# Turning the rows of hn with VectorE blocks and DMA writes instead of TensorE transposes

## The chip, the core and the metric

The kernel runs on one core of one Trainium2 chip. The core has five engines, each with an instruction queue of its own that it works through in order: TensorE (PE in the profile) multiplies matrices and transposes, VectorE (DVE) and ScalarE (ACT) work on rows of up to 128 partitions, GpSimd (POOL) does elementwise work beside them, and SyncE (SP) issues most of the DMA transfers. ScalarE can issue DMA transfers too; they stand in its queue between its computations. TensorE writes to PSUM, eight banks of 128 x 512 floats; everything else lives in SBUF or, outside the core, in DRAM. The metric is the device time of one execution in microseconds (us), as the median of several runs.

## The reference

All values are float32. With S = 2048 rows, D = 512 columns, 32 heads of 16 and a gate of 688 columns, the reference computes

```python
h  = x + A(layernorm(x))             # attention with wqkv, softmax, wo
h2 = h + B(layernorm(h))             # gated MLP that mixes rows

def B(x):
    z  = gelu(x @ w_in)              # 2048 x 1376
    z1 = z[..., :688]
    z2 = layernorm(z[..., 688:])
    g  = w_sp @ z2 + b_sp[:, None]   # 2048 x 2048 weights over the rows
    return (z1 * g) @ w_out
```

The change concerns the step from layernorm(h) to x @ w_in: the product needs the rows of layernorm(h), called hn, turned, with the 512 columns on the partitions.

## The kernel before

A float32 product is made of three products of float32r parts (`mm3`, lines 107 to 110): a value is split into hi, the rounded value, and lo, the rest (`split`, lines 97 to 105), and hi x hi, hi x lo and lo x hi are added in PSUM.

The work has four stages. First the rows of x are normalized and projected to q, k and v, which go to DRAM. Then comes attention, with scores, exponentials and weighted sums in an order that is written out by hand as strings (lines 42 to 57); its results o and their sums r go to DRAM too. The last 22 units of attention follow the string `FINAL` (line 44, `play_final`). In it the letter G is half a unit of scores with their exponentials, V a weighted sum, and H one product of the output projection: 36 letters H make the rows of h for the first three row blocks (`more_h`, lines 863 to 884), twelve products for each.

A row block has 128 rows. `h_rows` (line 616) says in which order the 16 row blocks are taken: 0, 1, 2, 8, 9, 10, 3, 11, 4, 12 and so on. I call the place in this order the row's index.

The middle stage begins at line 999 and has 16 rounds, k = 0 to 15 (line 1071). Before, round k does this, in the order of the program:

- `make_h` for the row with index k + 3 (while there is one): twelve products of o with wo on TensorE (L643), x added by VectorE (L653), the sum stored to h_scr by SP (L655), statistics (L657).
- `turn` for the row with index k + 1 (L1015): four 128 x 128 transposes of hn on TensorE into PSUM, then the split, hi on ScalarE (L100) and lo on VectorE (L105), into one of two places of the tile hT. The row with index 0 is turned ahead of the loop.
- `scale_h`: mean and variance of the new row, and one over its deviation, a chain of small VectorE operations.
- `make_z`, three pieces of the 1376 columns, each twelve products of hT with w_in (L108 to L110), followed by the GELU on ScalarE (L1034). Between the first two pieces stands the split of o for the row with index k + 4; between the second and third, VectorE's statistics of z2 (L1094) and hn of the new row, which ScalarE makes (L1097).
- `gate_z`: ScalarE issues the store of z1 (L1041), VectorE turns the statistics into scales (L1043, L119 to L135, L666), ScalarE applies them (L1046) and issues the store of z2 (L1047). SP issues `load_o` for the row with index k + 5: o, four loads of r (rc), and x (L623 to L629); GpSimd multiplies o by r (L630). For the row blocks 8 to 15, GpSimd also prepares parts of the later products (L1058 to L1066).

From line 999 on, the program's order is the order of every engine's queue; in attention this holds for all engines but GpSimd. SP works ahead of TensorE wherever its buffers and data allow. DMA transfers report their end through eight semaphores, which all issues use in turn; an issue waits until the transfer that used its semaphore before has landed.

PSUM in the middle stage: one bank for the products of h (`ph`), two for the transposes (`pt`), five for the pieces of z (`ps`).

The fourth stage mixes the rows with w_sp (seven products in place of eight, on sums and differences of blocks) and projects with w_out. It takes z1 and z2 from DRAM again.

Of the kernel before, what the change touches and what calls it, by code (L numbers as in the profile page):

```python
# [18 lines left out]
P = 128  # L19
# [41 lines left out]
def block_kernel(ctx: ExitStack, tc: tile.TileContext, x, wqkv, wo, w_in, w_sp4, b_sp, w_out, out):  # L61
# [28 lines left out]
    o_scr = dram.tile([D, S], F32, name="o_scr")  # L90
    r_scr = dram.tile([H, S], F32, name="r_scr")
    h_scr = dram.tile([S, D], F32, name="h_scr")
    z_scr = [dram.tile([S, FH], F32, name=f"z{i}_scr") for i in range(2)]
    s_scr = dram.tile([HB, P, HB, P], F32, name="s_scr")
    g_scr = [dram.tile([3, P, FC], F32, name=f"g{p}_scr") for p in range(HB)]
# [518 lines left out]
    wi4 = w_in.rearrange("(a p) c -> p a c", p=P)  # L614

    h_rows = [0, 1, 2, HB, HB + 1, HB + 2] + [sb + HB * i for sb in range(3, HB) for i in range(2)]
    os_, o2s, xrs, hns, hTs = {}, {}, {}, {}, {}

    def load_o(sb):

        c = slice(sb * P, (sb + 1) * P)
        o = e2.tile([P, DB, P], F32, name="o")
        nc.sync.dma_start(o, o_scr[:, c].rearrange("(d p) s -> p d s", p=P))  # L623
        rc = e2.tile([P, DB, P], F32, name="rc")
        for d in range(DB):
            nc.sync.dma_start(rc[:, d, :], r_scr[8 * d:8 * d + 8, c].rearrange(
                "h (o s) -> h o s", o=1).to_broadcast([8, DH, P]))
        xrs[sb] = e2.tile([P, D], F32, name="xr", bufs=3)
        nc.sync.dma_start(xrs[sb], x[c, :])  # L629
        nc.gpsimd.tensor_mul(o, o, rc)  # L630
        os_[sb] = o

    def split_o(sb, eh="act", el=None):
        o = os_.pop(sb)
        o2s[sb] = [e2.tile([P, DB, P], F32R, name=f"o2{i}", bufs=1) for i in range(2)]
        split(o2s[sb][0], o2s[sb][1], o, eh, el)
# [14 lines left out]
    def add_h(sb, acc, between=lambda: None):  # L651
        h = xrs[sb]
        nc.vector.tensor_add(h, acc, h)  # L653
        between()
        nc.sync.dma_start(h_scr[sb * P:(sb + 1) * P, :], h)  # L655
        hst[sb] = e2.tile([P, 6], F32, name="st")
        nc.vector.bn_stats(hst[sb], h)  # L657

    def scale_h(sb):
        mv = e2.tile([P, 2], F32, name="mv")  # L660
# [21 lines left out]
    with ExitStack() as at:  # L682
# [127 lines left out]
        def play_final(units):  # L810


            half = []
            for x in FINAL:
                if x == "G":
                    if not half:
                        unit = units.pop(0)
                        half.extend([unit, new_pt(), 0])
                        if unit[2] == 6 and sums_:
                            invert()  # L820
                        if len(units) in (7, 5):
                            load_o(h_rows[(7, 5).index(len(units)) + 3])
                    unit, pt, p = half
                    for step in score(unit, p, pt):
                        step()
                    half[2] += 1
                    if p:
                        waiting.append([(unit, pt, PLACES), 0])
                        half.clear()
                elif x == "V":  # L830
                    unit, *rest = waiting.pop(0)[0]
                    weigh(unit, *rest)
                    if unit[2] == NB - 1:
# [29 lines left out]
        def more_h(k):  # L863

            for _ in range(k):
                if not pieces:
                    sb = h_rows[len(hns)]
                    acc = later[0].tile([P, 512], F32, name="h")
                    pieces.extend([sb, acc, h_products(sb, acc)])
                sb, acc, products = pieces  # L870
                next(products)
                made[0] += 1
                if made[0] % (3 * DB):
                    continue
                pieces.clear()
                after = h_rows[len(hns) + 1]
# [5 lines left out]
                hns[sb] = e2.tile([P, D], F32, name="hn", bufs=3)  # L882
                nc.vector.tensor_scalar(hns[sb], xrs.pop(sb), mv[:, 0:1], rs,
                                        op0=ALU.subtract, op1=ALU.mult)

        made = [0]
        units = [(hg, qb, kb) for hg in range(HG) for qb in range(NQ) for kb in range(NB)]
# [3 lines left out]
        with tc.manual_schedule(engines={E.PE, E.Activation, E.DVE, E.SP}):  # L891
            end = len(units) - 2 * LEAD
            for n in range(0, end, 2):
                hg, qb, kb = units[n]
                if hg + 1 < HG and n % 64 < 24 and n % 4 == 0:
                    load_k(hg + 1, [n % 64 // 4])
                if hg + 1 < HG and n % 64 < 12 and n % 4 == 2:
                    load_d(hg + 1, [n % 64 // 4])
                if hg + 1 < HG and n % 64 == 30:
                    load_v(hg + 1)  # L900
                if kb == 2 and n // NB + 3 < HG * NQ:
                    load_q(n // NB + 3)
# [18 lines left out]
            load_o(h_rows[2])  # L921
            maxima.close()
# [77 lines left out]
    with ExitStack() as mid:  # L1000
        m2 = mid.enter_context(tc.tile_pool(name="mid_2", bufs=2))
        zs, zst = {}, {}
        hT = wc.tile([P, 2, 2, DB, P], F32R, name="hT", tag="w2")
        ph = mid.enter_context(tc.tile_pool(name="mid_ph", bufs=1, space=PSUM))
        pt = mid.enter_context(tc.tile_pool(name="mid_pt", bufs=2, space=PSUM))
        ps = mid.enter_context(tc.tile_pool(name="mid_ps", bufs=5, space=PSUM))

        turned = [0]

        def turn(sb):  # L1010

            hn = hns.pop(sb)
            tp = pt.tile([P, DB, P], F32, name="tp")
            for d in range(DB):
                nc.tensor.transpose(tp[:, d, :], hn[:, d * P:(d + 1) * P], ident)  # L1015
            hTs[sb] = [hT[:, i, turned[0] % 2] for i in range(2)]
            turned[0] += 1
            split(hTs[sb][0], hTs[sb][1], tp, "act")

        def new_z(sb):  # L1020
            zs[sb] = [m2.tile([P, FH], F32, name=f"z{i}", bufs=1 + 4 * i) for i in range(2)]
# [45 lines left out]

        w = [Slot(wc, f"w{i}") for i in range(3)]
        row = dict(enumerate(h_rows))
        turn(row[0])  # L1070
        for k in range(NB):
            sb, new = row[k], row.get(k + 3)
            if new is not None:
                make_h(new, (ph if k else ps).tile([P, 512], F32, name="acc"))
            if k + 1 < NB:
                turn(row[k + 1])
            if new is not None:
                mv, rs = scale_h(new)
                nb = minus_mean(e2, mv, rs)
# [9 lines left out]
            make_z(sb, *chunks[0])  # L1089
            if k + 4 < NB:  # L1090
                split_o(row[k + 4])
            make_z(sb, *chunks[1])
            for c in range(2):
                nc.vector.bn_stats(zst[sb][:, c, :], zs[sb][1][:, c * FC:(c + 1) * FC])  # L1094
            if new is not None:
                hns[new] = e2.tile([P, D], F32, name="hn", bufs=3)
                nc.scalar.activation(hns[new], xrs.pop(new), AF.Identity, bias=nb, scale=rs)  # L1097
            for c in chunks[2:]:
                make_z(sb, *c)
            hTs.pop(sb)  # L1100
            gate_z(sb, lambda: k + 5 < NB and load_o(row[k + 5]))
            if not k:
                invert()
            if k == NB - 5:
# [354 lines left out]
```

## Time and profile before

| what | us |
|---|---|
| median of 3 runs | 1803.45 (1803.33 to 1804.55) |
| the profiled execution's own time | 1802.38 |
| its span, first to last instruction | 1800.6 |
| the middle stage, round 0 to round 15 | 1351.36 to 1513.97 of the span |

The profile is of one execution. Its page gives the busy time of each engine; a chain of waits that is followed back from the last instruction; and groups of equal instructions with what their engine waited for. The timeline lists single instructions: start in us from the beginning of the span, duration, engine, line of the kernel, operation, and the tiles that are written and read (`hT<-tp`: hT from tp). In brackets stands the engine's idle time before it and what ended it. ACTq and SPq are the queues of ScalarE and SP; a `DMA_DIRECT2D` there is the issue of a transfer, not the transfer itself, and isn't counted as busy time. Rounds 0 to 12 of the middle stage last 10.67 us each, with round 0 a little longer; rounds 13 and 14 have no row of h to make and last 7.91.

### The profile page before, as it was taken

The numbers are of one execution on the slowest core, as the hardware profiler recorded it, in microseconds if no ns is written. First come the engines' busy times: TensorE is split into PE (matmuls) and PEld (weight loads), VectorE is DVE, ScalarE is ACT, GpSimd is POOL, SyncE is SP. The second block draws the span as 40 slices with busy tenths as digits, with TensorE's granted clock in tenths as the row PEclk, the third lists the DMA queues.
The fourth block names the chain that finished last, engine by engine and source line by source line (L and its number), as shares of the span: only waits on it lengthen the run. The fifth ranks groups of instructions, "written<-read, shape, count | busy, mean of one in ns | idle before, by whom it ended". The sixth has DMA issues, their size and how long they took to land.

```text
span 1800.6 us, 36057 instructions
## 1 busy us (share of the span) xinstructions
PE 1793.1 (100%) x13371; PEld 1050.6 (58%) x13371; DVE 1500.0 (83%) x3034; ACT 1378.4 (77%) x2674; POOL 218.4 (12%) x299
## 2 busy tenths in 40 slices
PE   9999999999999999999999999999999999999999
PEld 6876444444444444444444444444448889999998
DVE  6487999999999999999999999999936676778664
ACT  3224999999999999999999999999994445334231
POOL 2241000011010100000000000000110754001111
PEclk9999999999999999999999999999999999999999
DMA  6677111221120111021012011100134554668562
GB/s 199 192 194 182 43 26 27 49 56 30 36 59 19 51 39 26 20 50 35 14 36 44 24 30 38 26 15 15 40 74 143 168 176 151 216 208 278 184 197 91
DMA packets 148184, 157.54 MB, mean 87 GB/s; under 512 B 63032, under 2 KB 93256, under 8 KB 146664
## 3 DMA queue, kind: packets, MB, share of 16 engines
q1 hardware_dynamic: 143224, 143.82, 29.6%
q10 hardware_dynamic: 4752, 11.41, 1.6%
q8 instruction: 105, 1.72, 0.4%
q14 instruction: 71, 0.58, 0.1%
q0 software_dynamic: 32, 0.01, 0.0%
HBM read 99.69 MB, written 54.56 MB: 86 GB/s over the span
## 4 chain that ended last, share of the span: by engine, by line
PE 99%; DVE 1%; DMA 0%; issue 0%; ACT 0%; DVEq 0%
PE pv L726 30%; PE s L700 10%; PE s L237 9%; PE m L700 9%; PE m L237 7%; PE acc L108 6%; PE acc L110 6%; PE acc L109 6%; PE g L110 4%; PE g L109 4%; PE g L108 4%; PE acc L643 2%; PE tp L1319 1%; PE h L643 1%; PE acc L1340 0%; PE tp L1015 0%
## 5 line engine op out<-in xcount | busy, mean ns | idle before, releaser
L704 ACT ACTIVATE pt<-s 128x512 f32<-128x512 f32 (+1 forms) x1149 | 668.5, 632 | 3.4 <-PE s L700 3.0
L726 PE MATMUL pv<-pt,vst 128*32 128x256 f32 (+1 forms) x6048 | 595.2, 467 | 0.0
L242 DVE TENSOR_REDUCE mx<-s 128x1 f32<-128x512 f32 x826 | 539.6, 682 | 42.3 <-PE s L237 34.4
L704 ACT ACTIVATE pt<-m 128x512 f32<-128x512 f32 x855 | 500.3, 616 | 0.2 <-PE m L700 0.2
L242 DVE TENSOR_REDUCE mx<-m 128x1 f32<-128x512 f32 x682 | 452.3, 682 | 28.3 <-PE m L237 21.2
L700 PE MATMUL s<-qst,kst 50*128 50x512 f32 x1193 | 418.5, 437 | 0.0
L237 PE MATMUL s<-kst,qst 48*128 48x512 f32 x963 | 343.7, 421 | 0.0
L700 PE MATMUL m<-qst,kst 50*128 50x512 f32 x855 | 340.1, 440 | 0.0
L237 PE MATMUL m<-kst,qst 48*128 48x512 f32 x794 | 290.8, 423 | 0.0
L700 PEld LDWEIGHTS s<-qst,kst 50*128 50x128 f32 x1193 | 187.4, 184 | 145.0 <-DVE mx L242 91.0
L726 PEld LDWEIGHTS pv<-pt,vst 128*32 128x32 f32 x6048 | 120.4, 108 | 217.6 <-issue 208.5
L700 PEld LDWEIGHTS m<-qst,kst 50*128 50x128 f32 x855 | 146.2, 184 | 129.4 <-DVE mx L242 88.9
L237 PEld LDWEIGHTS s<-kst,qst 48*128 48x128 f32 x963 | 166.8, 184 | 40.4 <-issue 12.8
L237 PEld LDWEIGHTS m<-kst,qst 48*128 48x128 f32 x794 | 137.1, 184 | 41.7 <-issue 15.2
L247 ACT ACTIVATE ab<-s 128x512 f32<-128x512 f32 x167 | 100.4, 601 | 14.2
L102 POOL CAST mparts<-nm 128x16 fp32r<-128x16 f32 x32 | 6.3, 196 | 861.3 <-DVE nm L255 861.3
L251 DVE CUSTOM_DVE_ANT_0 ab<-s,ab 128x512 f32<-128x512 f32 x137 | 93.2, 680 | 5.1 <-PE s L237 5.1
L955 ACT ACTIVATE ws<-a 128x512 fp32r<-128x512 f32 x80 | 45.7, 621 | 48.7 <-PE g L110 23.8
L251 DVE CUSTOM_DVE_ANT_0 ab<-m,ab 128x512 f32<-128x512 f32 x112 | 76.2, 680 | 4.9 <-PE m L237 4.9
L237 PE MATMUL s<-dst,qst 48*128 48x512 f32 x167 | 79.6, 477 | 0.0
L1034 ACT ACTIVATE z<-acc 128x464 f32<-128x464 f32 (+2 forms) x64 | 27.5, 456 | 63.5 <-PE acc L110 63.5
L108 PE MATMUL acc<-wi,hT 128*128 128x464 f32 (+2 forms) x196 | 72.8, 371 | 0.0
(219 smaller groups left out, 2586.9 us busy)
## 6 DMA issues: line engine op xcount, KB each, us to landing
a<-in_w_sp SPq DMA_DIRECT2D x80, 256.0 KB
qst<-q_scr SPq DMA_DIRECT2D x192, 64.0 KB
z_scr<-z ACTq DMA_DIRECT2D x32, 344.0 KB
kst<-k_scr SPq DMA_DIRECT2D x42, 256.0 KB
k_scr<-part SPq DMA_DIRECT2D x16, 512.0 KB
q_scr<-part SPq DMA_DIRECT2D x16, 512.0 KB
z<-z_scr SPq DMA_DIRECT2D x14, 344.0 KB
b<-z_scr SPq DMA_DIRECT2D x24, 172.0 KB
```

The costliest lines, as they stand in the source:

```text
L108: nc.tensor.matmul(ps, lh, rh, start=first, stop=False)
L109: nc.tensor.matmul(ps, lh, rl, start=False, stop=False)
L110: nc.tensor.matmul(ps, ll, rh, start=False, stop=last)
L237: nc.tensor.matmul(acc, q[r, p, c], keys[r, p], start=True, stop=True)
L242: nc.vector.reduce_max(at(t, e if t else e - 1), acc, axis=AX.X)
L247: nc.scalar.activation(ab[0], acc, AF.Relu)
L251: nc.vector.tensor_tensor_reduce(ab[0], acc, ab[0], 1.0, LOW, ALU.add, ALU.max, at(0, 0))
L643: yield nc.tensor.matmul(acc, o2[b][:, d, :], wo2[a][:, d, :], start=i == 0, stop=i == 3 * DB - 1)
L700: nc.tensor.matmul(out, kst[hg % 2][r, p, kb * P:(kb + 1) * P], qst[hg * NQ + qb][r, p, :], start=True, stop=True)
L704: nc.scalar.activation(out, scores, AF.Exp, scale=DH ** -0.5)
L726: nc.tensor.matmul(pv[0][32 * j:32 * j + 32, cols], vst[hg % 2][:, c:c + 32], pt[:, places[t, p], cols], start=kb == 0, stop=kb == NB - 1 ...
L955: nc.scalar.activation(hi, src, AF.Copy)
```

## The change

TensorE's transposes of hn go. In their place each row block is turned in two steps. VectorE transposes the 128 x 512 tile in blocks of 32 x 32 (`flip`): afterwards, row 32 i + r and columns 32 j to 32 j + 31 of the tile z hold column 32 j + r of rows 32 i to 32 i + 31. Four DMA writes, one for each i, put these pieces of 32 floats (128 bytes) at their places in a DRAM tile ht_scr, whose rows are the columns of hn; 2048 pieces in all. Later SP fetches the turned block from there in one transfer (`fetch_turned`), and it is split into hi and lo as before (`split_turned`).

For the rows with index 0 to 2, which are made in attention, VectorE transposes and SP issues the writes right behind the store of h. Rows 0 and 1 are fetched in `play_final`, at the units with 13 and 3 left, and row 0 is split by VectorE when the second row of h is complete. For the rows made in rounds 0 to 12, ScalarE's queue issues the four writes, behind the store of z2, and SP fetches the row with index k + 2 at the end of round k, behind `load_o`. The split for the row with index k + 1 stands in round k between the first and second piece of z, behind the split of o. The turned copy shares the three buffers of hn. The five PSUM banks for z become seven, as no bank holds transposes any more.

```diff
+    ht_scr = dram.tile([D, S], F32, name="ht_scr")
...
+    def flip(sb, hn):
+
+        z = e2.tile([P, D], F32, name="hz", tag="hn", bufs=3)
+        nc.vector.transpose(z, hn)
+        q = 32
+
+        def write(e=nc.sync):
+            for i in range(P // q):
+                c = sb * P + q * i
+                e.dma_start(ht_scr[:, c:c + q].rearrange("(j r) c -> r j c", r=q),
+                            z[q * i:q * i + q, :].rearrange("r (j c) -> r j c", c=q))
+
+        return write
+
+    def fetch_turned(sb, pool, **slot):
+
+        raws[sb] = pool.tile([P, DB, P], F32, name="ht", **slot)
+        nc.sync.dma_start(raws[sb], ht_scr[:, sb * P:(sb + 1) * P].rearrange("(a p) s -> p a s", p=P))
+
+    def split_turned(sb, eh=None):
+
+        hTs[sb] = [hT[0][:, i, turns[0] % 2] for i in range(2)]
+        turns[0] += 1
+        split(hTs[sb][0], hTs[sb][1], raws.pop(sb), eh)
...
+                        if len(units) in (13, 3):
+                            fetch_turned(h_rows[(13, 3).index(len(units))], e2, tag="rc")
...
+                if made[0] == 6 * DB:
+                    split_turned(h_rows[0])
...
-                nc.vector.tensor_scalar(hns[sb], xrs.pop(sb), mv[:, 0:1], rs,
+                hn = e2.tile([P, D], F32, name="hn", bufs=3)
+                nc.vector.tensor_scalar(hn, xrs.pop(sb), mv[:, 0:1], rs,
                                         op0=ALU.subtract, op1=ALU.mult)
+                flip(sb, hn)()
...
-        pt = mid.enter_context(tc.tile_pool(name="mid_pt", bufs=2, space=PSUM))
-        ps = mid.enter_context(tc.tile_pool(name="mid_ps", bufs=5, space=PSUM))
-
-        turned = [0]
-
-        def turn(sb):
-
-            hn = hns.pop(sb)
-            tp = pt.tile([P, DB, P], F32, name="tp")
-            for d in range(DB):
-                nc.tensor.transpose(tp[:, d, :], hn[:, d * P:(d + 1) * P], ident)
-            hTs[sb] = [hT[:, i, turned[0] % 2] for i in range(2)]
-            turned[0] += 1
-            split(hTs[sb][0], hTs[sb][1], tp, "act")
+        ps = mid.enter_context(tc.tile_pool(name="mid_ps", bufs=7, space=PSUM))
...
-        turn(row[0])
...
-            if k + 1 < NB:
-                turn(row[k + 1])
...
             if k + 4 < NB:
                 split_o(row[k + 4])
+            if k + 1 < NB:
+                split_turned(row[k + 1], "act")
             make_z(sb, *chunks[1])
...
-                hns[new] = e2.tile([P, D], F32, name="hn", bufs=3)
-                nc.scalar.activation(hns[new], xrs.pop(new), AF.Identity, bias=nb, scale=rs)
+                hn = e2.tile([P, D], F32, name="hn", bufs=3)
+                nc.scalar.activation(hn, xrs.pop(new), AF.Identity, bias=nb, scale=rs)
+                write = flip(new, hn)
...
-            gate_z(sb, lambda: k + 5 < NB and load_o(row[k + 5]))
+
+            def meanwhile():
+                if new is not None:
+                    write(nc.scalar)
+                if k + 5 < NB:
+                    load_o(row[k + 5])
+                if k + 2 < NB:
+                    fetch_turned(row[k + 2], m2)
+
+            gate_z(sb, meanwhile)
```

The tile hT is now made ahead of `play_final`, since row 0 is split there.

More of the change, by code (lines that the diff above doesn't have):

```diff
@@ L616, in block_kernel @@
     h_rows = [0, 1, 2, HB, HB + 1, HB + 2] + [sb + HB * i for sb in range(3, HB) for i in range(2)]
-    os_, o2s, xrs, hns, hTs = {}, {}, {}, {}, {}
+    os_, o2s, xrs, hTs = {}, {}, {}, {}
     def load_o(sb):
@@ L657, in add_h @@
         nc.vector.bn_stats(hst[sb], h)
+    def flip(sb, hn):
[15 more added lines that the diff above has]
+        split(hTs[sb][0], hTs[sb][1], raws.pop(sb), eh)
+    raws, turns, hT = {}, [0], []
     def scale_h(sb):
@@ L866, in more_h @@
                 if not pieces:
-                    sb = h_rows[len(hns)]
+                    sb = h_rows[made[0] // (3 * DB)]
                     acc = later[0].tile([P, 512], F32, name="h")
@@ L875, in more_h @@
                 pieces.clear()
-                after = h_rows[len(hns) + 1]
+                if made[0] == 6 * DB:
+                    split_turned(h_rows[0])
+                after = h_rows[made[0] // (3 * DB)]
                 o = os_.pop(after)
@@ L881, in more_h @@
                 mv, rs = scale_h(sb)
-                hns[sb] = e2.tile([P, D], F32, name="hn", bufs=3)
-                nc.vector.tensor_scalar(hns[sb], xrs.pop(sb), mv[:, 0:1], rs,
+                hn = e2.tile([P, D], F32, name="hn", bufs=3)
+                nc.vector.tensor_scalar(hn, xrs.pop(sb), mv[:, 0:1], rs,
                                         op0=ALU.subtract, op1=ALU.mult)
+                flip(sb, hn)()
         made = [0]
@@ L921, in block_kernel @@
             load_o(h_rows[2])
+            hT.append(wc.tile([P, 2, 2, DB, P], F32R, name="hT", tag="w2"))
             maxima.close()
@@ L1002, in block_kernel @@
         zs, zst = {}, {}
-        hT = wc.tile([P, 2, 2, DB, P], F32R, name="hT", tag="w2")
         ph = mid.enter_context(tc.tile_pool(name="mid_ph", bufs=1, space=PSUM))
-        pt = mid.enter_context(tc.tile_pool(name="mid_pt", bufs=2, space=PSUM))
-        ps = mid.enter_context(tc.tile_pool(name="mid_ps", bufs=5, space=PSUM))
-        turned = [0]
-        def turn(sb):
-            hn = hns.pop(sb)
-            tp = pt.tile([P, DB, P], F32, name="tp")
-            for d in range(DB):
-                nc.tensor.transpose(tp[:, d, :], hn[:, d * P:(d + 1) * P], ident)
-            hTs[sb] = [hT[:, i, turned[0] % 2] for i in range(2)]
-            turned[0] += 1
-            split(hTs[sb][0], hTs[sb][1], tp, "act")
+        ps = mid.enter_context(tc.tile_pool(name="mid_ps", bufs=7, space=PSUM))
         def new_z(sb):
```

## The prediction

> **What bounds the kernel now.** I read the page first, then the chain of work that ended last, then the stage the change touches, round by round.
>
> ```profile
> span 1800.6 us, 36057 instructions
> PE 1793.1 (100%) x13371; PEld 1050.6 (58%) x13371; DVE 1500.0 (83%) x3034; ACT 1378.4 (77%) x2674; POOL 218.4 (12%) x299
> PEclk9999999999999999999999999999999999999999
> PE 99%; DVE 1%; DMA 0%; issue 0%; ACT 0%; DVEq 0%
> ```
>
> The chain is TensorE's from end to end (99%), at a granted clock of 0.9 or more in every slice. So an instruction taken off TensorE should shorten the run by the time that it holds the chain, provided that nothing else then comes last. The table of stretches shows the middle stage (from the end of attention to the first product of the token mixing), then one round of it, in its columns PE, PEld, DVE, ACT and POOL busy, clock, DMA share:
>
> ```profile
> 1351.36:1513.97 162.61, 162.61 (x809) 144.48 (x809) 109.11 (x352) 69.99 (x125) 88.00 (x101) 1.00 0.53 160
> 1405.35:1416.02 10.67, 10.67 (x53) 9.40 (x53) 7.32 (x25) 4.50 (x8) 10.15 (x13) 1.00 0.48 158
> ```
>
> TensorE is full for all 162.61 us. VectorE has 3.3 us to spare in a round of 10.67, ScalarE 6.2, the DMA engines about half. The chain by time shows what the transposes hold:
>
> ```profile
> 1351.36 0.59 PE tp L1015 x4
> 1405.35 2.76 PE acc L643 x12
> 1408.11 0.43 PE tp L1015 x4
> 1408.55 0.21 PE acc L108
> ...
> 1416.02 2.77 PE acc L643 x12
> ...
> 1490.76 0.44 PE tp L1015 x4
> 1491.19 0.21 PE acc L108
> ```
>
> **What goes.** The four transposes of a row block hold the chain 0.44 us (0.59 for the first, part of which is the filling that any first product has). 16 row blocks x 0.44 = 7.0 us. A round falls from 10.67 to 10.23. ScalarE's and VectorE's splits of hT stay; they move behind the first piece of z and read SBUF.
>
> **What comes, ScalarE.** Rounds 0 to 12 put four DMA issues into ScalarE's program, behind the store of z1. ScalarE works in order, so behind them wait the GELU of the next round's first piece, the splits of o and hT, the GELU of the second piece; then VectorE's statistics, and again ScalarE's scaling of z1. Rows of round 5's end and round 6 (ScalarE, then VectorE):
>
> ```profile
> 1418.15 0.33 ACTq L1047 DMA_DIRECT2D z_scr<-z  x1
> 1421.79 0.56 ACT L1034 ACTIVATE z<-acc 128x464 f32<-128x464 f32 x1 [1.93 <-PE acc L110]
> 1422.24 0.62 ACT L100 ACTIVATE o<-o 128x512 fp32r<-128x512 f32 x1
> 1424.23 0.60 ACT L1034 ACTIVATE z<-acc 128x224 f32<-128x224 f32 x2 [1.36 <-PE acc L110]
> 1424.72 0.82 ACT L1097 ACTIVATE hn<-xr,nb,rs_r 128x512 f32<-128x512 f32 x1
> 1417.15 0.97 ACT L1046 ACTIVATE z<-z,nb,rs_r 128x688 f32<-128x688 f32 x1 [0.53 <-DVE nb L666]
> 1413.94 0.94 DVE L1094 BATCH_NORM_STATS2 zst<-z 128x6 f32<-128x344 f32 x2 [0.96 <-ACT z L1034]
> 1414.91 0.21 DVE L1043 BATCH_NORM_AGGREGATE zmv<-zst 128x2 f32<-128x12 f32 x1
> 1416.90 0.21 DVE L666 TENSOR_SCALAR nb<-rs_r,zmv 128x1 f32<-128x1 f32 x1
> ```
>
> What do four issues cost? No issue of this shape exists. Near ones:
>
> ```profile
> 1483.97 0.93 SPq L961 DMA_DIRECT2D a<-in_w_sp  x2
> 1420.40 2.47 SPq L626 DMA_DIRECT2D rc<-r_scr  x4
> L285 SPq DMA_DIRECT2D qst<-mturned x256: 610/610/1058, 143.0 to 1313.4; - x128
> 683.47 1.79 SPq L195 DMA_DIRECT2D raw<-v_scr  x2
> ```
>
> One after another, 256 KB loads cost 0.47 each, the rc loads 0.62, the 2 KB writes of 128-byte pieces 0.61 (longest 1.06). A load of raw is 2048 pieces of 128 bytes, as many as the four writes of a row together, and two of them take 1.79. So W, the four issues, lies between 4 x 0.33 = 1.3 and 4 x 1.06 = 4.2; I take 2.0, between the first two rows, which are spread over the engines as the writes should be.
>
> **VectorE** gets one 128x512 transpose in 32x32 blocks per row. The trace has only 128x32 ones, and other passes over 128x512:
>
> ```profile
> L281 DVE STREAM_TRANSPOSE mturned<-mparts x32: 199/204/211, 142.7 to 1307.2; 128x32 f32<-128x32 f32 x32
> L242 DVE TENSOR_REDUCE mx<-s 128x1 f32<-128x512 f32 x826 | 539.6, 682 | 42.3 <-PE s L237 34.4
> ```
>
> Bounds: 0.20, and 16 x 0.20 = 3.3 if each 32 columns paid in full. I take 0.68, a pass over 512 elements, since the other small VectorE rows (0.21 for one element) say that the 0.20 is mostly fixed.
>
> Does this close a loop longer than 10.23? From GELU to GELU: first GELU to second split 0.45, two splits 0.62 + 0.60, second GELU 0.60; its end at 1424.83 to the end of the statistics, by the same spacing as 1413.94 to 1414.88, 0.73; transpose 0.68; aggregate to nb (1414.91 to 1417.11) 2.20; scaling 0.97; store 0.33; W 2.0. Sum 9.2. That is under 10.23, so ScalarE returns in time: the store of z1 ends 2.46 us into round 6; with the round 0.44 shorter and the transpose 0.68 longer that becomes about 3.1 in the next round, W ends at 5.1, and the first GELU's products are there at 5.77 - 0.44 = 5.3. Cost 0, hidden under TensorE's products. hn and its turned copy share three buffers; the one that hn takes was read by writes issued a round before: no wait. GpSimd, 10.15 busy in rounds 3 to 5, still fits 10.23; three such rounds make its product of o late by tenths. Spare: the split of o (6.4 by then) is wanted by TensorE at 10.23, so ScalarE may run 3.8 us late before TensorE waits.
>
> **DMA.** Per row 2048 writes of 128 bytes and 512 reads of 512 bytes. How long the pieces take to land:
>
> ```profile
> 688.99 1.04 POOL L197 COPY vst<-raw 128x1024 f32<-128x1024 f32 x1 [12.33 <-DMA raw<-v_scr]
> 1419.55 0.33 SPq L655 DMA_DIRECT2D h_scr<-xr  x1
> 1422.98 0.39 SPq L629 DMA_DIRECT2D xr<-in_x  x1
> ```
>
> 4096 such pieces, issued from 683.47, had landed by 688.99: 5.5 us, so 2048 take under 5.5 and I take 3 from the last issue. These are reads from DRAM; no 128-byte write to DRAM stands in the trace, so I keep 3 to 12 us. The writes end at 5.1 of a round and land at 8. SP's fetch comes behind h_scr, o, rc and xr of that round (done about 7.4) and waits until 8; SP's next store is due at 3.5 of the next round, so nothing behind it suffers. The fetch lands by 11 (o, the same shape, needs no longer), and the split that wants it comes at 6.4 of the round after, which is 16.6: 5 us spare before ScalarE waits, 3.8 more before TensorE does. Cost 0.
>
> The Trainium skill (DMA: Bandwidth & Descriptors, Specifications) speaks against the 128-byte writes: under 512 bytes a transfer is read, modified and written back. The trace's 128-byte reads do not test it; it is the reason given there for the late landing among the rivals.
>
> **The start.** Row 2's four writes go on SP ahead of the last stores of o, and behind a VectorE transpose ending near 1352.2, against stores that began at 1352.96: they begin at about 1354.2, 1.3 us later, and so does the load of o for row block 5:
>
> ```profile
> 1352.96 0.32 SPq L747 DMA_DIRECT2D o_scr<-o  x1
> 1359.60 2.56 SPq L626 DMA_DIRECT2D rc<-r_scr  x4
> 1367.83 1.29 POOL L630 TENSOR_TENSOR o<-o,rc 128x512 f32<-128x512 f32 x1 [21.39 <-DMA rc<-r_scr]
> 1369.15 0.63 ACT L100 ACTIVATE o<-o 128x512 fp32r<-128x512 f32 x1 [0.19 <-POOL o L630]
> 1373.31 2.77 PE acc L643 x12
> ```
>
> Its split ended at 1369.78 and TensorE used it at 1373.31, which moves up by 3 x 0.44. Spare 3.5 - 1.3 = 2.2 us, lo part about 1.5, against 1.3 later: 0 to 1 us of waiting, once; I take 0.3. At the tail, rounds 13 and 14 last 7.91 - 0.44 = 7.5 us, so a late ScalarE catches up less there; with W = 2.0 I find the last splits half a us ahead of TensorE and take 0.1. Row 0 is split by VectorE during attention, where ScalarE's exponentials set the pace; 0.
>
> **Sum.** 7.0 - 0.3 - 0.1 = 6.6. Profiled execution: 1802.38 (span 1800.6 and 1.8 around it) gives 1795.8; the median of the runs is 1.07 above it, so 1803.45 - 6.6 = **1796.8**. What is late next is still TensorE.
>
> **Rivals.**
>
> A. *ScalarE's queue becomes the bound; slower.* The loop is 7.2 + W. From W = 3.0 on it exceeds 10.23 and ScalarE falls behind each round; the lead of 3.8 us goes first, then TensorE waits. With W = 4.2 (each issue as long as the longest 1.06) the loop is 11.4: 13 rounds x 1.2 = 15.6, less 3.8, is 11.8 lost against 7.0 gained: **1808**. For it: ScalarE's writes (3.1 to 5.1 of a round) coincide with SP's loads of o; and an issue waits for the transfer that had its semaphore eight issues before, which can be an rc load: these landed 5.7 us after their issue (1362.16 to 1367.83), so at about 12.7 of a round, and the writes begin at 13.3. Against it:
>
> ```profile
> 1498.91 1.37 SPq L961 DMA_DIRECT2D a<-in_w_sp  x3
> 1499.30 0.35 ACTq L1041 DMA_DIRECT2D z_scr<-z  x1
> ```
>
> a ScalarE issue in the midst of three of SP's took 0.35, not 0.33, and the three 0.46 each. Chance 0.14. The Trainium skill (Perfetto Trace Analysis, Per-engine timelines) has a mechanism for this rival: the block that generates descriptors is shared by two issuing engines and locked while one uses it. With four of SP's 0.62 between ScalarE's four, W would be 4.5 and the time about 1812; the 0.35 above speaks for a lock that is held briefly.
>
> B. *The writes land late and the gain is eaten.* Past about 9 us (5 spare over the 3 taken, and a little) ScalarE is late, past 12 TensorE waits for hT. A row is made three rounds before its use, so each further us adds a third of one to a round, 4 us in all; landing at 13 to 14 leaves **1801 to 1804**, about no change. For it: strided small writes are the one thing the trace doesn't show. Chance 0.08.
>
> C. *The chain of o at the start, and the tail, cost more.* Each of the next rounds begins with ScalarE late and it recovers 1.0 us a round at most, so 1 to 4 us are lost: **1798 to 1801**. Chance 0.15.
>
> D. *The freed time is not freed*: the 0.44 would return as a slower first product after the switch from o to h. Against it: the product behind the transposes takes 0.21 in the chain like the others, and 0.43 + 2.76 + 36 x 0.21 make up the round. Included in C's chance.
>
> **How the numbers follow.** The forecast has 0.60 (1796 to 1798), C 0.15, B 0.08, A 0.14, and 0.03 is for more than 7.0, if the first row's 0.59 goes whole and nothing waits. A measurement here can tell about 0.2%, 3.6 us, from no change: faster means under 1799.8. The forecast, the 0.03 and two thirds of C are faster: 0.73. The rest of C, B and the lightest of A are within: 0.13. Slower, past 1807: 0.14. The range from 1795.5 (the 7.2 of all transposes, and half a us) to 1804.5 takes in the forecast, C and B, some 0.83; A's upper bound of W stays out.
>
> **What would show it.** Right: no transposes of hn on TensorE in the middle stage, rounds of 10.23 with TensorE at 100%, four issues on ScalarE in 1.6 to 2.5 us, one VectorE transpose per row near 0.68. Wrong by A: TensorE idle before the products of o or z, released by ScalarE, and issues of 0.8 us and more. Wrong by B: ScalarE's split of hT waiting for the fetch. Wrong by C: a TensorE gap near the start of round 2 or 15. The forecast falls if any engine's loop passes 10.23.

## The result and the profile after

| | us | |
|---|---|---|
| before | 1803.39 | median of 6 runs |
| after | 1852.5 | median of 6 runs; ratio 1.0264, 95% interval 1.0236 to 1.0291 |
| predicted | 1796.8 | 1795.5 to 1804.5 |
| profiled execution of after | 1853.13 | span 1851.3 |

The change costs 49 us where 6.6 were to be gained. (Of the runs below, one execution of run 3 took 5762.62 us at a mean granted clock of 0.352; it is left out of that run's time.) Lines of the page of after (span, busy time, granted clock by slice, the chain's shares):

```profile
span 1851.3 us, 36088 instructions
PEclk9999999999999999999999999999999889999999
PE 89%; DMA 5%; DVE 2%; issue 1%; ACT 1%; SPq 1%; ACTq 0%; POOL 0%; DVEq 0%; POOLq 0%
```

The chain is no longer TensorE's alone: 11% of it lies elsewhere, against 1% before. The table of stretches (us; PE, PEld, DVE, ACT, POOL busy with counts; clock; DMA share; GB/s) shows the stage and one round of it:

```profile
1351.00:1565.00 214.00, 177.04 (x753) 147.63 (x750) 123.93 (x368) 66.20 (x126) 91.24 (x102) 0.91 0.61 157
1385.59:1399.68 14.09, 10.72 (x42) 8.53 (x41) 7.62 (x25) 4.20 (x8) 1.28 (x1) 0.88 0.78 178
```

A round lasts 14.09 us instead of 10.67. TensorE is idle for a quarter of it, and what it does is slower: at a granted clock of 0.88 on the mean of the round, its busy time includes twelve products of h that take 4.89 us, not 2.76. The chain through that round, in order of time, and then ScalarE's timeline in the same round, two later ones, and one without loads of o:

```profile
1384.16 0.97 ACT z L1066
...
1385.16 0.39 ACTq L1067
...
1385.59 5.00 DMA ht_scr<-hz
...
1390.62 1.66 ACTq L669
...
1392.32 0.16 ACT z L1054
...
1392.78 0.63 ACT o L101
...
1393.45 4.89 PE acc L644 x12
...
1400.58 5.57 DMA rc<-r_scr
```

```profile
1385.59 6.69 ACTq L669 DMA_DIRECT2D ht_scr<-hz  x4
1392.32 0.56 ACT L1054 ACTIVATE z<-acc 128x464 f32<-128x464 f32 x1 [7.19 <-DMA ht_scr<-hz]
...
1399.68 6.15 ACTq L669 DMA_DIRECT2D ht_scr<-hz  x4
...
1504.26 8.02 ACTq L669 DMA_DIRECT2D ht_scr<-hz  x4
...
1540.48 2.22 ACTq L669 DMA_DIRECT2D ht_scr<-hz  x4
```

These are steps of the prediction's loop: store of z2, the four writes, GELU, split of o; TensorE waits for the last. W, from the start of the first issue to the end of the fourth, is 6.80 on the mean of rounds 0 to 9 (4.63 to 8.02) and 2.43 in rounds 10 to 12, where SP loads no o. Of the 6.80, the four issues themselves take 2.65 on the mean; the other 4.15 lie between them. What is waited for there is a landing: for 5.00 us the chain stands on one of ScalarE's own writes. From the trace's semaphore events the whole burst from 1399.68 on can be set out. The last column says how long the semaphore that an issue uses had been free:

```
start   issue  queue   transfer         semaphore  landed   free for
1399.68  0.47  ScalarE ht_scr<-hz   #1      S101   1404.13    4.19
1399.93  0.59  SP      rc<-r_scr    #1      S110   1404.38    4.02
1400.19  1.05  ScalarE ht_scr<-hz   #2      S114   1405.92    1.59
1400.58  0.79  SP      rc<-r_scr    #2      S112   1406.15    4.29
1401.41  1.07  SP      rc<-r_scr    #3      S113   1407.78    2.10
1402.53  0.57  SP      rc<-r_scr    #4      S115   1408.17    1.38
1403.20  0.40  SP      xr<-in_x             S116   1408.80    0.28
1403.80  0.31  ScalarE ht_scr<-hz   #3      S118   1409.22    0.02
1404.15  1.67  ScalarE ht_scr<-hz   #4      S101   1409.56    0.02
```

Write #3 wants the semaphore of the load of o, issued at 1399.50, and goes 0.02 us after its landing at 1403.78. Write #4 is exactly eight transfers behind write #1, wants the same semaphore, and goes 0.02 us after that has landed. Eight transfers are under way, and the next has to wait for the one whose semaphore it is to use. Of ScalarE's 52 writes 21 begin this close behind such a landing: 10 behind a load of o, 8 behind one of ScalarE's own writes. In the kernel before, none of the 81 issues between 1372 and 1470 us began within 0.12 us of the landing before it; the semaphores had been free for 4.82 us on the median and 1.04 at the least. A round had 9 transfers then (h, o, four rc, xr, z1, z2) and has 14 now (four writes and a fetch more).

Of the 50.7 us between the spans (1851.3 - 1800.6), the stores of z2 tell when they come. Before (first two rows, rounds 10 and 12), and after (rounds 0, 10 and 12); round 0's store before stood at 1366.57:

```profile
1471.53 0.33 ACTq L1047 DMA_DIRECT2D z_scr<-z  x1
...
1493.04 0.33 ACTq L1047 DMA_DIRECT2D z_scr<-z  x1
```

```profile
1371.10 0.37 ACTq L1067 DMA_DIRECT2D z_scr<-z  x1
...
1520.39 0.34 ACTq L1067 DMA_DIRECT2D z_scr<-z  x1
...
1540.10 0.34 ACTq L1067 DMA_DIRECT2D z_scr<-z  x1
```

4.5 us are lost by round 0, and 44.3 from there to round 10's store, with ten bursts of writes between (4.4 each). By round 12, where W is 2.43, 1.8 are won back; 3.6 are lost after.

W is not all of it. From the start of one burst to the next, these ten rounds last 14.89 us on the mean: W and 8.09 more. The part beside W is 7.40 to 7.45 behind the bursts of rounds 0, 1, 2 and 6, and 8.25 to 8.83 behind the six others. In each of these six, one of VectorE's splits (of hT, once of o) takes 1.42 to 1.78 us instead of 0.68: it begins while an instruction of GpSimd runs, and ends 0.54 or 0.55 us after that one. The split behind round 2's burst, and the one behind round 7's with GpSimd's product of o:

```profile
1407.59 0.68 DVE L106 TENSOR_TENSOR hT<-ht,hT 128x512 fp32r<-128x512 f32 x1
...
1480.95 1.32 POOL L631 TENSOR_TENSOR o<-o,rc 128x512 f32<-128x512 f32 x1 [0.56 <-DMA ht_scr<-hz]
...
1481.03 1.78 DVE L106 TENSOR_TENSOR hT<-ht,hT 128x512 fp32r<-128x512 f32 x1
```

In the kernel before, where the split of hT read PSUM (L105, `hT<-tp`), it took 0.67 to 0.69 us all 16 times, eleven of them beside GpSimd. As long as ScalarE's loop sets the pace, this is some 0.7 us a round, by the estimate 8.09 - 7.4.

### The profile page after: what moved, and what is told of

Its sections match the earlier page's. It is cut to its first block, busy times and chain, and to the rows that moved or that the text cites. A ratio compares the mean times of both kernels' runs of the same rounds, so it can differ in the third digit from the quotient of the medians.

```text
span 1851.3 us, 36088 instructions
## 1 busy us (share of the span) xinstructions
PE 1807.1 (98%) x13307; PEld 1053.3 (57%) x13307; DVE 1516.4 (82%) x3051; ACT 1373.9 (74%) x2673; POOL 220.5 (12%) x299
## 4 chain that ended last, share of the span: by engine, by line
PE 89%; DMA 5%; DVE 2%; issue 1%; ACT 1%; SPq 1%; ACTq 0%; POOL 0%; DVEq 0%; POOLq 0%
PE pv L754 29%; PE s L728 10%; PE s L238 9%; PE m L728 8%; PE m L238 7%; PE g L111 4%; PE g L110 4%; PE g L109 4%; PE acc L109 4%; PE acc L111 3%; PE acc L110 3%; DMA ht_scr<-hz 3%; PE acc L644 1%; DMA o<-o_scr 1%; PE tp L1348 1%
## 5 line engine op out<-in xcount | busy, mean ns | idle before, releaser
L644 PE MATMUL acc<-wo,o 128*128 128x512 f32 x156 | 54.0, 501 | 33.7 <-ACT o L101 32.9
```

The costliest lines, as they stand in the source:

```text
L644: yield nc.tensor.matmul(acc, o2[b][:, d, :], wo2[a][:, d, :], start=i == 0, stop=i == 3 * DB - 1)
```

## Experiments: what about the writes costs the time

Four theories went in: **Q** (the issues hold ScalarE, for semaphores), **P** (128-byte pieces are slow in themselves), **V** (VectorE's transpose and the moved splits close the loop), and, inside Q, whether the issues wait for SP's loads or for their own first write.

**Run 1**, without ScalarE's writes:

```diff
-                if new is not None:
-                    write(nc.scalar)
...
-                    fetch_turned(row[k + 2], m2)
+                    fetch_turned(row[k + 2], m2, o_scr if k else ht_scr)
```

> The four writes that ScalarE issues in rounds 0 to 12 are left out; VectorE still turns the row, and SP fetches a block of the same shape from o_scr in place of ht_scr, so the rows from index 3 on are wrong. Theory Q (the four issues hold ScalarE's queue, some 6.2 us a round, so that its loop is 7.2 + 6.2 = 13.4) and theory P (the 128-byte pieces are slow in themselves) both expect the loss to go: 1795 to 1798 us, TensorE at 99 to 100%. Theory V (VectorE's transpose and the splits that moved close the loop, whatever the writes do) expects 1840 or more.

1809.0 us, ratio 1.0039 (1.0024 to 1.0054). V falls: 43 of the 49 us hang on the writes. But both Q and P missed by 11 us: with 10 transfers a round, SP's own issues meet the limit (19 of 96 issues between 1372 and 1470 began within 0.12 us of the landing before), and rc lands in 6.83 us on the mean, not 5.30. How the rest of the 11 divides between rounds, start and tail was not taken apart here; runs 8 to 13 do that for a variant with 11.

**Run 2**, the same bytes in 512-byte pieces:

```diff
+                if e is nc.scalar:
+                    e.dma_start(ht_scr[P * i:P * i + P, sb * P:(sb + 1) * P].rearrange("(r j) s -> r j s", j=DB),
+                                z[q * i:q * i + q, :].rearrange("r (j s) -> r j s", s=P))
+                    continue
```

> ScalarE still issues four writes for a row with the same bytes, but in pieces of 512 bytes instead of 128, so that the pieces land in other places of ht_scr and the rows from index 3 on are wrong. Theory P (small pieces) expects four issues in about 2.0 us and 1795 to 1800 us. Theory Q (waits in the issues, whatever their pieces) expects four issues in 5.5 to 7 us in the rounds with loads of o, and 1845 to 1855 us.

1830.19 us, ratio 1.0149 (1.0134 to 1.0164): between the two, and both theories as written are wrong. The issues of two rounds, one after the other, on ScalarE's timeline of this run:

```profile
1386.63 5.25 ACTq L670 DMA_DIRECT2D ht_scr<-hz  x4
...
1399.31 4.75 ACTq L670 DMA_DIRECT2D ht_scr<-hz  x4
```

W is 5.19 on the mean of rounds 0 to 9, against 6.80. The pieces matter through the landing: the wide writes land 4.14 us after their issue on the mean of all 52, the narrow ones 4.96, and a semaphore is held that long. Of the 5.19, the issues take 2.56 and the waits between them 2.64, against 2.65 and 4.15 in the kernel after: the small pieces cost waiting, not issuing. Waits remain at both sizes. The round shown is 12.68 = W + 7.43; the one of the kernel after is 14.09 = 6.69 + 7.40. In the kernel after, the loop is W + 7.4 where VectorE's splits take their 0.68 us.

**Run 3**, the writes ahead of the scaling; **run 4**, the writes on SP, behind the loads of o and the fetch:

```diff
         nc.scalar.dma_start(z_scr[0][rows, :], z[0])
+        early()
```

with `early` being `write(nc.scalar)`, and for run 4

```diff
-                if new is not None:
-                    write(nc.scalar)
                 if k + 5 < NB:
                     load_o(row[k + 5])
                 if k + 2 < NB:
                     fetch_turned(row[k + 2], m2)
+                if new is not None:
+                    write(nc.sync)
```

> The same four writes stand one place earlier in ScalarE's queue: behind the store of z1 and ahead of the scaling, where VectorE's chain of small operations keeps ScalarE waiting for some 2 us. SP's loads of o of the round before should be over there. Theory Q-o (the issues wait for semaphores that SP's loads of o hold at the time) expects four issues in 2 to 3 us, hidden in that gap, and 1796 to 1800 us. Theory Q-w (they wait mostly for their own first write, whose semaphore the fourth takes again) expects four issues in 5 us or more and 1830 to 1850 us.

> SP issues the four writes, behind the loads of o and ahead of the fetch of the next row; ScalarE issues only its two stores. Theory Q expects ScalarE's loop back at 7.2 us, TensorE at 99 to 100% and 1795 to 1799 us, as SP has some 5 us to spare in a round of 10.23. A rival (SP stands in the waits instead, and the next loads of o come late) expects 1805 to 1830 us, with TensorE or GpSimd waiting for o or rc.

Run 3: 1823.54 us, ratio 1.0113 (1.0096 to 1.0130); neither half of Q as priced: waits for SP's transfers and for own writes both occur. Run 4: 1846.0 us, ratio 1.0232 (1.0217 to 1.0248). (Its expectation has the writes ahead of the fetch of the next row; in the edit they stand behind it.) This is the rival, and more than it allowed. ScalarE's loop is free of the four issues, and still nothing is won, as the same wait now stands in SP's queue. The table of waits of its SP queue between 1372 and 1470, and its chain:

```profile
SPq L627 <- DMA z_scr<-z: 23.6, 4, 6.5
```

```profile
1404.08 6.51 DMA z_scr<-z
...
1410.65 0.34 SPq L630
...
1411.04 3.25 DMA ht<-ht_scr
...
1414.85 0.58 ACT z L1054 x2
```

SP issues the load of x (L630) only once a store that *ScalarE* issued has landed, 0.06 us after it, and the fetch and ScalarE's next work stand behind it. The two queues are coupled through the semaphores, in either direction.

## Experiments: the count of transfers

From here the theories are **S** (the count against eight semaphores) and **D** (the load of the added bytes on the DMA engines or DRAM). Run 5 takes three transfers out of a round without moving a byte less; run 6 adds five transfers of 512 bytes to the kernel *before*.

```diff
-    r_scr = dram.tile([H, S], F32, name="r_scr")
+    r_scr = dram.tile([8, NB, DB, P], F32, name="r_scr")
...
-        for d in range(DB):
-            nc.sync.dma_start(rc[:, d, :], r_scr[8 * d:8 * d + 8, c].rearrange(
-                "h (o s) -> h o s", o=1).to_broadcast([8, DH, P]))
+        nc.sync.dma_start(rc.rearrange("p d s -> p (d s)"), r_scr[:, sb].rearrange(
+            "h d s -> h (d s)").rearrange("h (o x) -> h o x", o=1).to_broadcast([8, DH, DB * P]))
```

> The kernel after, with r_scr stored in another order (head in its group of eight, row block, group, row), so that the reciprocals of a row block are one load of 256 KB instead of four of 64 KB: 11 transfers a round instead of 14, the same bytes. Theory S (all transfers share eight semaphores; an issue waits for the landing of the one eight before it, which 14 a round bring within reach and 9 did not) expects most waits in the issues to go, ScalarE's four writes in 2 to 3.5 us, and 1798 to 1815 us. Theory D (the DMA engines or DRAM are loaded by the added 128-byte and 512-byte pieces) expects no more than a few us: 1840 to 1852.

```diff
+                if new is not None:
+                    for i in range(4):
+                        nc.scalar.dma_start(small[5 * k + i:5 * k + i + 1, :], ident[i:i + 1, :])
...
+                if k + 2 < NB:
+                    nc.sync.dma_start(small[5 * k + 4:5 * k + 5, :], ident[4:5, :])
```

> The kernel before, TensorE's transposes and all, plus five transfers a round of one row of 512 bytes each that nobody reads: four that ScalarE issues where the kernel after issues its writes, one that SP issues where it fetches the turned row. Theory S (eight semaphores in turn) expects the added count alone to hold ScalarE and SP: 1815 to 1850 us. Theory D (load of the added bytes) expects 1803 to 1806, and theory V (VectorE's transpose, the moved splits) the same.

Run 5: 1815.96 us, ratio 1.0069 (1.0054 to 1.0084), just above what S gave: three transfers fewer give 36 of the 49 us back. Run 6: 1816.88 us, ratio 1.0073 (1.0057 to 1.0090): TensorE's transposes are all there, 2.5 KB a round are added, and it costs 14 us. From its table of waits (1330 to 1540 us; total, times, longest): ScalarE's split of the turned row stands behind the small transfers. In seven of the 13 rounds the fourth of them begins 0.02 us after the landing that it waits for.

```profile
ACT hT L101 <- DMA small<-ident: 33.3, 9, 8.4
```

Both are as S has it and against D. What run 5 leaves is a second, smaller effect. Its ScalarE and SP side by side in one round:

```profile
1402.96 3.69 ACTq L668 DMA_DIRECT2D ht_scr<-hz  x4
```

```profile
1402.97 0.58 SPq L626 DMA_DIRECT2D rc<-r_scr  x1
1403.60 0.54 SPq L629 DMA_DIRECT2D xr<-in_x  x1
```

No issue of these four waited for a semaphore (free for 3.60, 0.66, 3.59 and 1.38 us), and yet they took 0.63, 0.99, 0.91 and 1.05 us, 3.69 for the four, against 2.2 to 2.7 where SP loads no o. W + 7.4 is 11.1 then, still over 10.23; to the next burst it took 12.64, in part because GpSimd held up VectorE's split again (1.41 us). The rule of the Trainium skill that the prediction weighed (Perfetto Trace Analysis, Per-engine timelines: two issuing engines share the block that generates descriptors) agrees in direction; but SP's two issues here end by 1404.14 while ScalarE's go on at 0.9 to 1.05, so this run doesn't show that the sharing is the cause.

**Runs 7 and 8** repeat runs 4 and 3 with the single load of rc.

> SP issues the four writes, as in the fourth run, and the reciprocals are one load: 11 transfers a round, ScalarE only its two stores. Theory S expects SP's waits to shrink and the loads of o to come in time again: 1797 to 1812 us, well under the fourth run's 1846.0. Theory D expects 1835 to 1846.

> ScalarE's writes between the store of z1 and the scaling, as in the third run, and the reciprocals one load. Theory S expects 1796 to 1806 us, under the third run's 1825.0: with 11 transfers a round the one eight before an issue lies most of a round back. Theory D expects 1820 to 1825.

Run 7: 1816.63 us, ratio 1.0075 (1.0060 to 1.0091), 29 us under run 4, though above what was expected. Run 8: 1805.86 us, ratio 1.0016 (1.0007 to 1.0025), 18 under run 3. D falls in both. The chain of run 8 has rounds of the forecast length:

```profile
1417.35 2.76 PE acc L643 x12
...
1427.59 2.76 PE acc L643 x12
...
1437.84 2.76 PE acc L643 x12
```

10.24 and 10.25, TensorE without a gap. So 0.43 a round is won, as foreseen, and what keeps the run above the kernel before lies at the stage's two ends.

## Experiments: the start, the tail, and a version that is faster

**Run 9** is the control, the kernel before with the single load.

> A control: the kernel before with only the reciprocals as one load, 6 transfers a round instead of 9. Before, no issue in rounds 2 to 12 waited for a semaphore (the one eight before had landed 3.6 us or more earlier), so theory S expects no change: 1802.5 to 1804.5 us. If the single load were itself worth the tens of us of the runs before, it would show here as 1795 or less.

1803.43 us, ratio 1.0001 (0.9992 to 1.0011): worth nothing by itself. (The 3.6 us of the expectation is not the least in the trace: five issues of round 2 and one of round 10 found their semaphore free for 1.04 to 2.27 us only. None waited.)

**Run 10** came from ScalarE's timeline in run 8 and in the kernel after. This row is run 8's; in the kernel before this table load stood at 1357.78 and waited for TensorE:

```profile
1361.59 1.28 ACT L1054 ACT_TABLE_LOAD   x1 [8.07 <-DMA sums<-o]
```

The ht tiles were taken from the pool of z. I infer that its z tiles thereby came to lie where o and its sums wait to be stored at the end of attention, so that the first GELU waits for the last store; the edit tests it.

```diff
         m2 = mid.enter_context(tc.tile_pool(name="mid_2", bufs=2))
+        mh = mid.enter_context(tc.tile_pool(name="mid_h", bufs=2))
...
-                    fetch_turned(row[k + 2], m2)
+                    fetch_turned(row[k + 2], mh)
```

> The eighth run with the two ht tiles of the middle stage in a pool of their own, opened behind the pool of z, so that z no longer lies where o and its sums wait to be stored when attention ends. Its rounds 2 to 10 already last 10.23 us; I expect the start to lose what the first GELU waited for there: 2 to 4 us less than 1805.86, that is 1802 to 1804. A rival (the start is late because the four writes of row 2 delay the stores and loads of o on SP) expects no change, 1805 to 1806.5.

1803.23 us, ratio 0.9999 (0.9991 to 1.0008), 2.6 under run 8, as expected; the table load stands at 1357.75 and waits for TensorE again. **Run 15** made this edit alone in the kernel after:

> The kernel after with only one thing altered: the ht tiles of the middle stage in a pool of their own, so that the first GELU no longer waits for the last store of the sums of o (8.83 us in the kernel after). If the start were a loss of its own that adds to the rounds', 2 to 5 us less than 1852.5; if ScalarE's loop of 13.5 to 15 us a round sets the pace anyway, the lateness of the start still counts once, so also 2 to 5 less; no change would say that something else held TensorE there.

1850.12 us, ratio 1.0259 (1.0245 to 1.0273), against 1.0264. The table load comes at 1356.98 there instead of 1362.77, but the difference of the medians lies within the intervals; at that place it can't be told from no change.

**Runs 11 and 12**, the tail, and row 2's writes:

```diff
-                if k + 2 < NB:
+                if k + 2 < NB - 1:
                     fetch_turned(row[k + 2], mh)
...
-            ... (lambda: write(nc.scalar)) ...
+            ... (lambda: write(nc.scalar if k + 5 < NB else nc.sync)) ...
...
             if k == NB - 4:
                 a11 = ask(0, 0, 0, "xr")
+                fetch_turned(row[NB - 1], mh)
```

> The tenth run, and at the tail: SP issues the writes of rounds 11 and 12, where it has no loads of o, and the fetch of the last row stands ahead of the stores of s, which wait for GpSimd. In the eighth run the middle stage lost some 4 us between round 11 and its end there. I expect 3 to 5 us less than the tenth run: 1797.5 to 1800.5 us, the first version under the kernel before. A rival (GpSimd's own work sets the end of the stage, whoever issues) expects no change against the tenth run.

> The eleventh run, and the four writes of row 2 behind the last stores of o on SP instead of ahead of them. By the prediction's step for the start these writes put off the loads of o by some 2 us; if that still costs, 0.5 to 2 us less than the eleventh run; if the wait of the first GELU was all of it, the same within 0.5 us.

Run 11: 1801.64 us, ratio 0.9991 (0.9982 to 1.0000), 1.6 under run 10 and not the 3 to 5 expected. Run 12: 1802.65 us, ratio 0.9995 (0.9986 to 1.0004), no difference that can be told. Two rows of run 11's tail say what was missed, ScalarE waiting for row 14's fetch, and GpSimd for loads of w_sp that had been put behind the writes:

```profile
1492.62 0.63 ACT L101 ACTIVATE hT<-ht 128x512 fp32r<-128x512 f32 x1 [2.64 <-DMA ht<-ht_scr]
```

```profile
1493.54 2.83 POOL L1009 TENSOR_TENSOR s<-a,a 128x512 f32<-128x512 f32 x2 [5.54 <-DMA a<-in_w_sp]
```

**Runs 13 and 14** mend these two, with row 2's writes as in run 11 and as in run 12:

```diff
-                if k + 2 < NB - 1:
+                if k + 2 < NB - 2:
                     fetch_turned(row[k + 2], mh)
...
+            if k == NB - 4:
+                a11 = ask(0, 0, 0, "xr")
             gate_z(...)
...
-            if k == NB - 4:
-                a11 = ask(0, 0, 0, "xr")
-                fetch_turned(row[NB - 1], mh)
+            if k in (NB - 5, NB - 4):
+                fetch_turned(row[k + 3], mh)
```

> The eleventh run with SP's queue at the tail in another order: the fetch of row 14 behind its own writes in round 11 instead of behind those of row 15, and the last two loads of w_sp for GpSimd's sums ahead of row 15's writes. In the eleventh run round 12 began 4.0 us earlier than in the kernel before, and 2.7 of them were lost again by the end of the stage, where ScalarE waited 2.64 us for the fetch of row 14 and GpSimd 5.54 for those loads. If these waits are the loss, 1 to 2.5 us less than 1801.64: 1799 to 1800.6. If the tail is set by GpSimd's and VectorE's own work, 1801 to 1802.

> The thirteenth run, and row 2's writes behind the last stores of o. Against the thirteenth run: the same within 1 us, as between the twelfth and the eleventh.

Run 13: 1799.33 us, ratio 0.9978 (0.9968 to 0.9987). Run 14: 1799.61, ratio 0.9979 (0.9970 to 0.9988). Run 13 is as expected, and the two do not differ. Both lie under the kernel before by 0.2%, with intervals that end below 1. Run 13's page, and two pieces of its chain:

```profile
span 1796.0 us, 36017 instructions
PE 99%; DVE 0%; issue 0%; ACT 0%; DVEq 0%
```

```profile
1352.37 2.96 PE acc L643 x12
...
1509.08 0.40 PE g L109
```

The chain is TensorE's again. The stage, from the first product to the first of the token mixing, takes 156.7 us; before, from the first transpose at 1351.36 to 1513.97, it took 162.6. So 5.9 of the 7.0 come out in the stage, and 4.6 in the span of this execution.

## Why the prediction was wrong

It fell by rival A, at 0.14, and beyond the price set for it.

- **The step that failed is W**, under "What comes, ScalarE": the term 2.0, bounds 1.3 to 4.2. It measured 6.80 in the rounds with loads of o, and 2.43 in the three without. The bounds were made of issue times only, and as such they held: issuing took 2.65 of the 6.80. The other 4.15 is waiting for semaphores, which the sum has at nothing. The price of such a wait is set by a landing, 4.4 to 6.4 us after the issue in the burst above, not by an issue's longest 1.06.
- The semaphore wait was named in rival A, but looked for at the wrong distance. It was placed at an rc load landing at 12.7 of a round against writes at 13.3, which is a position in a round of 9. With 14 in a round the eighth transfer back is in the same burst: the load of o, and the first of the same four writes. The count of transfers in flight was never made.
- The row set against rival A, a ScalarE issue of 0.35 amid three of SP's, was true of one issue with few transfers under way. Run 5 has the case that mattered: four in a row beside SP's, 3.69 us without a semaphore wait in the round shown.
- **The loop itself was right in four of ten rounds.** 7.2 + W with a turning point at W = 3.0; it measured 7.4 + W there, and 8.25 to 8.83 + W in the six others. With the mean W, 7.4 gives 14.2 us a round; the mean round took 14.89. The step behind the rest is that the splits "move behind the first piece of z and read SBUF", at no cost: VectorE's split of hT was 0.68 from SBUF alone and up to 1.78 when GpSimd was at work. (The store and the scaling that this loop calls z1's are z2's, L1047 and L1046, as its rows show; the sum stays the same.)
- Right: the freed 0.44 a round (10.24 in runs 8 and 13), so rival D falls; VectorE's transpose, 0.69 against 0.68; and that rival B's late fetch wasn't the bound: the writes landed 4.96 us after their issue on the mean (2.21 to 8.06), and one split of hT alone waited for the fetch, 2.1 us in the tail.
- **The start**, 0.3, was mis-sized too: 4.5 us by round 0's store. The prediction followed the load of o; the first GELU waited for the stores of o, by run 10 because of where the ht tiles came from, which no row of before could show. Run 10 won 2.6 us by it; in the kernel after, run 15 could not tell the gain from none.
- **The tail**, 0.1, likewise: 3.6 us in the kernel after. Runs 11 and 13 show what it can be: fetches and loads standing behind writes on SP.
- TensorE's idleness can be paid twice. Where it had to wait, its clock fell (0.91 in the stage, 1.00 before): the trace has eight stretches at 0.5 there, of 3.4 or 6.8 us each, 37.5 us in all, and in one of them h's twelve products took 4.89 us, on the chain. The prediction counted waits only. How much of the 49 us this is was not measured; ScalarE's loop has no product in it. The Trainium skill (TensorE: Matmul & The Clock Gate, What's actually happening) has the clock halved after an idle window of about 3.4 us; the lengths of these stretches agree.

## What to carry to other kernels

Before transfers are added to a loop, count those of one round, multiply by the time from issue to landing, and divide by the semaphores that they share. Here the estimate is 14 x 5 us / 8 = 8.8 us of a round of 10.2 on an even spread, and bursts do the rest. The issue that then waits can be on another engine's queue than the transfer it waits for, so moving the new transfers to a queue with time to spare (run 4) needn't help, while merging old ones (run 5) can. The wait does not show in the time of a single issue: it lies between issues, and a timeline row that merges four of them (6.15 us) hides it. Set the start of each issue against the landing of the eighth transfer before it.

## What the runs showed of the hardware that had not been expected

- Five transfers a round of 512 bytes each cost 14 us in a kernel that TensorE bounded at 99% (run 6).
- Four issues that waited for no semaphore took 0.63 to 1.05 us each, 3.69 together, beside a burst on the other queue, and 2.2 to 2.7 together where SP loaded no o (run 5).
- A split by VectorE that read SBUF and began while an instruction of GpSimd ran took up to 1.78 us instead of 0.68, and ended 0.54 or 0.55 after it (kernel after); the same split from PSUM kept its 0.67 to 0.69 beside GpSimd (kernel before).
- A new tile in a pool delayed an unrelated one: the table load of the first GELU waited for stores of the stage before and came at 1361.59 (run 8) instead of 1357.78 (before); with a pool of its own for the tile it came at 1357.75 (run 10).
- 512-byte pieces instead of 128-byte ones, the same bytes, took the landing from 4.96 to 4.14 us and the time from 1852.5 to 1830.19 (run 2).
